# An adaLN block with sliding-window attention and a token MLP: Q's parity copies of two token groups by DMA, K1 and Q2 a group ahead, 20 more token blocks of B1 inside attention

## The chip, the cores and the metric

The kernel runs on one core of one Trainium2 chip. The metric is the device time of one execution in microseconds (us); the median of several executions stands for a kernel. The engines are TensorE (PE; PEld is its weight load), VectorE (DVE), ScalarE (ACT), GpSimd (POOL) and SyncE (SP), which here only issues DMAs.

## The reference

`x` is 2048 tokens by 512 features, bf16. A modulation vector gives six rows of 512.

```
sa, ca, ga, sb, cb, gb = split(silu(c) @ w_mod)
h = layernorm(x) * (1 + ca) + sa
q, k, v = split(h @ wqkv)                 # 32 heads of 16
p = softmax(q k^T * 16**-0.5, only 0 <= query - key < 256)
x = x + ga * ((p v) @ wo)
h = layernorm(x) * (1 + cb) + sb
u = gelu(layernorm(h)^T @ w1 + b1)        # mixes tokens: w1 is 2048 x 1792
x = x + gb * (u @ w2 + b2)^T              # w2 is 1792 x 2048
```

## The kernel before, in words

**Stages.** A prologue makes the modulation and the first projections. Attention follows, then the token MLP: "B1" multiplies the normalized rows `hb` with `w1`, "y" multiplies the result with `w2`.

**Attention** is cut into four token groups `tg` of 512 tokens, each into four head blocks `g8` of 8 heads, each into five units: 80 units in all, 20 per token group (`ul` = 0 to 19). Four units of a head block (k = 0, 1, 3, 4; kind A) hold one parity of the heads and half of the keys' pieces; unit k = 2 (kind C) holds the pieces that fill the rest of the window. In each unit TensorE makes scores into PSUM (`emit_scores`, L548, L555, L575, L585), ScalarE turns them into exponentials in two instructions (`emit_exp`, L598), and TensorE multiplies these with V (`av_a`, L609, from `VaugT`; `av_c`, L623, from `Vc`, after units k = 2 and 4). VectorE transposes the products (L655), GpSimd and VectorE normalize them into `OTd` (`norm_rest`).

**Q in two copies.** A 32-row piece of Q holds two heads of 16 rows. `QT[tg][g8]` has two copies of Q, one with only the even heads' rows, one with only the odd heads', zeros elsewhere. `qk_group` (L292 to L317) evacuates Q from PSUM into `qs` (VectorE, L309), then two masked copies are made from it (L313, GpSimd but for one). `qpool` has two buffers for each `g8`.

**Dense groups.** Beside its own products TensorE gets at most one dense group per unit, of 16 matmuls (`dense`, L267), through one PSUM buffer `dn`: projections of V, Q and K, transposes of the normalized x, the output projection of a token block (`wo_group`), and parts of B1 (`part_group`). `plan(tg)` (L760) lays each group on a unit: `at[ul]`. Token group tg's own V blocks 2 and 3 come in units 0 and 1, its K and Q of head blocks 1 to 3 in units 2 to 8; the next token group's transposes, first Q and K and V blocks in units 11 to 18; the `wo` groups of the previous token group's four blocks in units 6, 7, 9 and 10. Behind a `wo` group, `ln23` gives three steps for VectorE and GpSimd that end in `hb[tb]`. Steps of this kind wait in `chains`; `fill` puts them between VectorE's fixed work by the planner's costs in `clock`, which also follows GpSimd.

**Parts of B1 in attention.** `part_group(fc, k)` multiplies four token blocks (4k to 4k + 3) of `hb` with the `w1` columns of chunk `fc` (128 of the 1792). `PART = (6, 7, 8, 9)`: these four chunks get their token blocks 0 to 7 in units 12 to 19 of token group 3, and the sum is kept in `part[fc]` in SBUF. After attention they start at token block 8 (L1047), and `emit_gelu` adds the part (L973). The other chunks do all 16 token blocks after attention (`emit_b1_group0_sc`, L961, for chunks 0 to 5; L1050 for the rest).

**Order in one unit** `u` (L881 to L914): first half's exponential; scores of unit u + 1; the products of unit u - 1, if these close a head block's half (k = 2 or 4); the dense group; the second exponential; the group's evacuation (`evac`); the other products; at last `at_unit`, which issues the unit's DMAs. Every engine works through its own list in this order.

**DMAs.** All are issued by SyncE, in program order. `copies_for` (L637) copies V for head block g8 from `VaugT` into the other 64 partitions of `Vc`, three copies each (L633), SBUF to SBUF; `at_unit` issues them for head block 0 in unit 0, and for blocks 1, 2 and 3 in units 3, 4 and 5. From unit 2 of token group 1 on, each unit issues one half row block of `w1` into `w1a` (20 loads for `NA` = 10 token blocks; `paced`, L408). The other token blocks (`w1b`, L946) and `w2` (L948) are loaded when attention's SBUF comes free.

Of the kernel before, what the change touches and what calls it, by code (L numbers as in the profile page):

```python
# [8 lines left out]
DT = mybir.dt  # L9
# [3 lines left out]
P = 128  # L13
# [3 lines left out]
DH = 16  # L17
# [3 lines left out]
ND = D // P  # L21
NF = F // P
EPS = 1e-5
SCORE_SCALE = DH ** -0.5
NA = 10
LIVE = 4
SLACK = 0.3

# [2 lines left out]
def kernel(  # L31
# [25 lines left out]
    dma = nc.sync  # L57
# [33 lines left out]
    hbpool = ctx.enter_context(tc.tile_pool(name="hbpool", bufs=1))  # L91
    hb = [hbpool.tile([P, D], DT.bfloat16, name=f"hb_{t}") for t in range(NT)]
    opool = ctx.enter_context(tc.tile_pool(name="opool", bufs=2))

    PART = (6, 7, 8, 9)
    ppool = ctx.enter_context(tc.tile_pool(name="ppool", bufs=1))
    part = {fc: ppool.tile([P, D], DT.float32, name=f"part{fc}") for fc in PART}
    wqpool = tc.alloc_tile_pool(name="wqpool", bufs=1)
# [66 lines left out]
    build_masks()  # L165


    qpool = tc.alloc_tile_pool(name="qpool", bufs=2)
    kpool = tc.alloc_tile_pool(name="kpool", bufs=1)
    vpool = tc.alloc_tile_pool(name="vpool", bufs=1)  # L170
    qspool = tc.alloc_tile_pool(name="qspool", bufs=2)
# [7 lines left out]
    QT = [[None] * ND for _ in range(NG)]  # L179
    KT = [[None] * ND for _ in range(NG)]  # L180
    VaugT = [None] * NG
    OTd = [[None] * ND for _ in range(NG)]
# [10 lines left out]
    nc.gpsimd.memset(ones[:], 1.0)  # L193


    for tg in range(NG):
        VaugT[tg] = Vring[tg % 2]
        for g8 in range(ND):
            KT[tg][g8] = Kring[tg % 2][:, g8, :]

# [91 lines left out]
    def qk_group(tg, g8, kind, pool):  # L292
        col0 = g8 * P + (D if kind == "k" else 0)

        def mms():
            pq = pool.tile([P, 4 * P], DT.float32, name="dn")
            for dc in range(ND):
                dense(
                    pq, lhsT=wqkv[:, dc, col0 : col0 + P], rhs=h1T[tg][:, dc, :],
                    start=(dc == 0), stop=(dc == ND - 1),  # L300
                )
            return pq

        def evac(pq):
            if kind == "k":
                nc.vector.tensor_copy(out=KT[tg][g8], in_=pq[:])  # L306
                return
            qs = qspool.tile([P, 4 * P], DT.bfloat16, name="qs")
            nc.vector.tensor_copy(out=qs[:], in_=pq[:])  # L309
            QT[tg][g8] = qpool.tile([P, 2, 4 * P], DT.bfloat16, name=f"QT{g8}")  # L310
            for n, m in enumerate((mask_even, mask_odd)):
                eng = nc.vector if (tg, g8, n) == (0, 1, 0) else nc.gpsimd
                eng.tensor_scalar(  # L313
                    out=QT[tg][g8][:, n, :], in0=qs[:], scalar1=m[:], scalar2=0.0, op0=ALU.mult, op1=ALU.add,
                )
            return 0.7 if (tg, g8) == (0, 1) else 1.4
        return mms, evac, (1.05 if (tg, g8, kind) == (0, 1, "q") else 0.7)  # L317
# [70 lines left out]
    with tc.manual_schedule():  # L388
# [6 lines left out]
            out=spread[:].rearrange("p (a b) -> p a b", a=4),  # L395
            in_=identity[0:32, 0:32].unsqueeze(1).to_broadcast([32, 4, 32]),
# [52 lines left out]
        for lo, hi, in_ in (  # L449
# [3 lines left out]
                out=mask_q[:, lo:hi, :], in_=in_.to_broadcast([P, hi - lo, 64]), func=ACT.Copy,  # L453
            )
        for half in range(2):
            part64 = slice(64 - 64 * half, 128 - 64 * half)
            nc.scalar.activation(
                out=Vc[half][part64, :, 0:8, :], func=ACT.Copy,
                in_=zero[part64, 0 : 8 * 2 * DH].rearrange("p (h d) -> p h d", d=2 * DH)
# [32 lines left out]
        for dc in range(ND):  # L492
            if dc < 2:
                nc.vector.tensor_scalar(
                    out=h1T[0][:, dc, :], in0=pts[dc], scalar1=modFM[:, 4 + dc : 5 + dc],
                    scalar2=modFM[:, dc : dc + 1], op0=ALU.mult, op1=ALU.add,
                )
            else:
                nc.scalar.activation(
                    out=h1T[0][:, dc, :], in_=pts[dc], func=ACT.Identity,  # L500
# [4 lines left out]
        for dc in (0, 2, 1, 3):  # L505
            for ps, col0 in ((pq, 0), (pk, D)):
                dense(
                    ps, lhsT=wqkv[:, dc, col0 : col0 + P], rhs=h1T[0][:, dc, :],
                    start=(dc == 0), stop=(dc == ND - 1),
                )  # L510
        QT[0][0] = qpool.tile([P, 2, 4 * P], DT.bfloat16, name="QT0")

        def q_half(n, m, lo, hi):
            nc.vector.tensor_scalar(
# [9 lines left out]
        mms, evac, _ = v_group(0, 0, ps_po, "po")  # L524
# [135 lines left out]
        def norm_rest(tg, g8):  # L660
            t2v = state["t2"][:].rearrange("p a (b c) -> p a b c", c=32)
            m = npool.tile([P, 4 * P], DT.bfloat16, name="merge")

            def quotient():
                zr = npool.tile([P, 2, 16, 1], DT.float32, name="zr")
                nc.vector.reciprocal(out=zr[:], in_=t2v[:, :, :, DH : DH + 1])  # L666
                nc.gpsimd.tensor_tensor(  # L667
                    out=m[:].rearrange("p (b a d) -> p a b d", a=2, d=DH), in0=t2v[:, :, :, 0:DH],
                    in1=zr[:].to_broadcast([P, 2, 16, DH]), op=ALU.mult,
                )  # L670
                return 1.06

            def back():
                OTd[tg][g8] = opool.tile([P, 4 * P], DT.bfloat16, name=f"OTd{g8}")
                nc.vector.transpose(out=OTd[tg][g8][:], in_=m[:])
            return [(quotient, 0.36), (back, 0.72)]

# [60 lines left out]


        def part_group(fc, k):  # L740
            def mms():
                assert done >= set(range(4 * k, 4 * k + 4))
                if k == 0:
                    part[fc, "ps"] = ps_dn.tile([P, D], DT.float32, name="dn")
                for sc in range(4 * k, 4 * k + 4):
                    dense(
                        part[fc, "ps"], lhsT=w1box["a"][:, sc, fc * P : (fc + 1) * P], rhs=hb[sc][:],
                        start=(sc == 0), stop=(sc == 7),
                    )
                return part[fc, "ps"]  # L750

            def evac(ps):
                if k == 1:
                    nc.vector.tensor_copy(out=part[fc][:], in_=ps[:])
            return mms, evac, 0.7 * k


        wo_next = iter(range(12))
# [1 line left out]
        def plan(tg):  # L760
            at, then = {}, {}

            def lay(ul, group):
                assert ul not in at, (tg, ul)
                at[ul] = group

            def qk(ul, g, g8, kind):
                lay(ul, qk_group(g, g8, kind, ps_dn))

            for n in (2, 3):  # L770
                lay(n - 2, v_group(tg, n, ps_dn))
            if tg == 0:
                for ul, g8, kind in ((2, 1, "q"), (3, 1, "k"), (4, 2, "q"), (5, 2, "k"), (6, 3, "q"), (7, 3, "k")):
                    qk(ul, tg, g8, kind)
                lay(8, bias_group(ps_dn))
                lay(13, bc_group(ps_dn))
                then[18] = [(lambda g=g: fold_wod(g), 0.0) for g in range(ND)]
            else:
                for ul, g8, kind in ((2, 1, "k"), (3, 2, "q"), (4, 2, "k"), (5, 3, "q"), (8, 3, "k")):
                    qk(ul, tg, g8, kind)  # L780
                for ul in (6, 7, 9, 10):
                    tb = next(wo_next)
                    lay(ul, wo_group(tb, ps_dn))
                    then[ul] = ln23(tb)
            if tg + 1 < NG:
                t0, t1, q0, v0, k0, q1, v1 = (10, 11, 12, 16, 14, 15, 18) if tg == 0 else (11, 12, 13, 14, 15, 17, 18)
                lay(t0, transpose_group(tg + 1, 0, ps_dn))
                lay(t1, transpose_group(tg + 1, 1, ps_dn))
                lay(v0, v_group(tg + 1, 0, ps_dn))
                lay(v1, v_group(tg + 1, 1, ps_dn))  # L790
                for ul, g8, kind in ((q0, 0, "q"), (k0, 0, "k"), (q1, 1, "q")):
                    qk(ul, tg + 1, g8, kind)
            else:
                for n, fc in enumerate(PART):
                    for k in range(2):
                        lay(12 + 2 * n + k, part_group(fc, k))
            return at, then
# [79 lines left out]
        mms, evac, _ = v_group(0, 1, ps_dn)  # L877
# [3 lines left out]
        for u, (tg, g8, k) in enumerate(units):  # L881
            ul = 5 * g8 + k
# [150 lines left out]
    with tc.tile_pool(name="gtmp", bufs=2) as gtmp:  # L1033
        for i, fc in enumerate(fgroups[1]):
            emit_gelu(pu1, i, fc, gtmp)
        pu1pool.release()
        for i, fc in enumerate(fgroups[0]):
            emit_gelu(pu0, i, fc, gtmp)
        ps_u = [
            tc.alloc_tile_pool(name=f"ps_u{n}", bufs=1, space=bass.MemoryType.PSUM, side="right")  # L1040
            for n in range(2)
        ]
        for n, fg in enumerate(fgroups[2:]):
            pu = ps_u[n % 2].tile([P, 2, D], DT.float32, name=f"pu{n % 2}")
            for sc in range(NT):
                for i, fc in enumerate(fg):
                    s0 = 8 if fc in PART else 0  # L1047
                    if sc < s0:
                        continue
                    nc.tensor.matmul(  # L1050
                        pu[:, i, :], lhsT=w1_of(sc, fc), rhs=hb[sc][:],
                        start=(sc == s0), stop=(sc == NT - 1),
                    )
            for i, fc in enumerate(fg):
                emit_gelu(pu, i, fc, gtmp)
        ps_u[1].release()
        ps_u[0].release()
    pu0pool.release()

    with tc.tile_pool(name="ftmp", bufs=3) as ftmp, tc.tile_pool(  # L1060
        name="ps_y0", bufs=4, space=bass.MemoryType.PSUM
# [61 lines left out]
```

## Time and profile before

| | |
|---|---|
| time, median of 3 runs | 265.92 us (264.77 to 267.12) |
| the profiled execution: its own time | 264.77 us |
| its span, first to last instruction | 263.0 us |
| busy, share of the span: PE / DVE / ACT / POOL | 92% / 64% / 62% / 49% |
| mean granted TensorE clock | 0.993 |
| token group 0 of attention | 13.6 to 50.7 us |
| token group 1 | 50.7 to 88.4 us |
| token group 2 | 88.4 to 127.05 us |
| token group 3 | 127.05 to 165.3 us |
| B1 after attention | 165.3 to 211.2 us |
| y | 211.2 to 263 us |

The token groups are cut where ScalarE begins the first exponential of each (40 exponentials per group). In the profile a line such as L598 is a line of the kernel; "out<-in" names the tiles; "[0.47 <-ACT et L598]" behind an instruction is the idle time of its engine ahead of it and what ended it. A busy TensorE is not one at its peak, since matmuls overlap. DMA-issuing instructions do not count as busy, so SyncE's queue (SPq) has views of its own.

### The profile page before, as it was taken

Reading aid. Unit: us, or ns where it says so; the run is one execution under the profiler, and the core shown is the slowest. Engines: PE = TensorE matmul, PEld = TensorE weight load, DVE = VectorE, ACT = ScalarE, POOL = GpSimd, SP = SyncE. Lnnn points to the kernel's source line nnn. Section 1 sums busy time; section 2 is a strip of 40 time slices with the busy share of each in tenths; the row PEclk is TensorE's granted clock in tenths of the full one; section 3 lists DMA queues with packets and bytes.
Section 4 is the critical chain, followed back from the end, with each engine's and each line's share of the span. In section 5 each row is a group of like instructions: output and inputs, shape, how many; then the busy total and the mean of one; then the engine's idle time right before and its main releaser. Section 6 shows DMA issues by size and latency. Waiting matters only on the chain.

```text
span 263.0 us, 11079 instructions
## 1 busy us (share of the span) xinstructions
PE 240.8 (92%) x4923; PEld 129.6 (49%) x4933; DVE 167.2 (64%) x353; ACT 164.3 (62%) x193; POOL 128.6 (49%) x218
## 2 busy tenths in 40 slices
PE   6988798899998879989899899999999999999994
PEld 2544455455555545555456455444444444444443
DVE  6678868875798697898786877789411001423444
ACT  6688998999999989999999999100082110000000
POOL 6104943699269998898995498954200000000000
PEclk9999979999999999999999999999999999999999
DMA  5949962134744342000122000999800000202021
GB/s 168 340 143 250 245 215 79 47 89 123 224 130 133 110 129 73 6 2 5 32 75 53 5 2 24 333 417 414 356 3 0 2 0 0 80 2 80 20 101 40
DMA packets 26084, 29.95 MB, mean 114 GB/s; under 512 B 3252, under 2 KB 23476, under 8 KB 26036
## 3 DMA queue, kind: packets, MB, share of 16 engines
q1 hardware_dynamic: 26036, 29.25, 35.4%
q8 instruction: 38, 0.62, 1.0%
q14 instruction: 10, 0.08, 0.1%
HBM read 22.55 MB, written 2.23 MB: 94 GB/s over the span
## 4 chain that ended last, share of the span: by engine, by line
PE 70%; DVE 18%; ACT 5%; issue 3%; DMA 2%; SPq 1%; ACTq 0%; DVEq 0%
PE dn L271 19%; PE py L1086 18%; PE pu L1050 8%; PE pu L964 7%; PE pss L548 5%; ACT et L598 5%; PE po L609 4%; PE po L623 3%; DVE t L655 3%; DVE qs L309 3%; DVE VaugT L287 2%; DMA wmod<-in_w_mod_dram 2%; PE pss L555 2%; DVE KT L306 2%; DVE x L370 1%
## 5 line engine op out<-in xcount | busy, mean ns | idle before, releaser
L598 ACT ACTIVATE et<-pss 128x1024 bf16<-128x1024 f32 (+1 forms) x160 | 143.8, 995 | 6.4 <-PE pss L555 5.1
L1086 PE MATMUL py<-guT,w2r 128*128 128x512 bf16 (+1 forms) x234 | 48.3, 366 | 0.2
L1065 DVE SCALAR_TENSOR_TENSOR o<-py,bFM,bc 128x512 bf16<-128x512 f32 (+1 forms) x17 | 11.7, 715 | 44.4 <-PE py L1086 44.4
L271 PE MATMUL dn<-h1T,wqkv 128*32 128x512 bf16 x496 | 33.1, 381 | 3.9 <-DVE VaugT L287 1.3
L1086 PEld LDWEIGHTS <-w2r 128*128 128x128 bf16 x238 | 23.3, 98 | 25.3
L548 PE MATMUL pss<-QT,KT 32*128 32x64 bf16 (+2 forms) x704 | 28.9, 238 | 5.8 <-ACT et L598 4.8
L655 DVE STREAM_TRANSPOSE t<-po 128x512 f32<-128x512 f32 x32 | 22.8, 711 | 11.4 <-PE po L623 11.2
L208 POOL TENSOR_TENSOR ln_rstd<-ln_ve,mhalf 128x1 f32<-128x1 f32 (+1 forms) x40 | 24.1, 602 | 5.7 <-DVE ln_ve L204 2.6
L204 POOL TENSOR_SCALAR ln_ve<-ln_mv 128x1 f32<-128x1 f32 (+1 forms) x38 | 9.1, 240 | 34.7 <-DVE ln_mv L226 17.6
L548 PEld LDWEIGHTS <-KT 32*128 32x128 bf16 x704 | 15.4, 92 | 21.3 <-issue 11.1
L609 PE MATMUL po<-et,VaugT 128*32 128x64 bf16 (+2 forms) x704 | 25.1, 241 | 0.0
L609 PEld LDWEIGHTS <-VaugT 128*32 128x32 bf16 x704 | 17.2, 96 | 11.0 <-issue 2.1
L271 PEld LDWEIGHTS <-wqkv 128*32 128x32 bf16 x512 | 13.1, 95 | 13.5 <-issue 6.0
L555 PE MATMUL pss<-mask_q,mask_k 32*128 32x256 bf16 (+1 forms) x256 | 19.2, 263 | 0.0
L667 POOL TENSOR_TENSOR merge<-t,zr 128x512 bf16<-128x512 f32 x16 | 17.0, 1060 | 3.2 <-DVE zr L666 3.2
L271 PE MATMUL dn<-wqkv,h1T 128*32 128x512 bf16 x240 | 15.7, 380 | 2.2 <-DVE VaugT L287 1.2
L975 ACT ACT_TABLE_LOAD x1 | 1.3, 1283 | 24.9 <-PE pu L964 24.9
L699 POOL TENSOR_TENSOR h<-h,bc 128x512 bf16<-128x512 bf16 x12 | 14.0, 1166 | 3.5 <-DVE h L695 3.5
L271 PE MATMUL dn<-wod,OTd 128*32 128x512 bf16 x192 | 12.6, 381 | 2.0 <-DVE KT L306 1.0
L700 POOL TENSOR_TENSOR h<-h,bc 128x512 bf16<-128x512 bf16 x12 | 13.9, 1155 | 0.9
L964 PE MATMUL pu<-hb,w1a 128*128 128x512 bf16 x58 | 13.2, 379 | 0.2 <-issue 0.2
L623 PE MATMUL po<-et,Vc 128*32 128x64 bf16 x960 | 13.0, 194 | 0.0
(113 smaller groups left out, 363.7 us busy)
## 6 DMA issues: line engine op xcount, KB each, us to landing
w2r<-in_B_w_dram SPq DMA_DIRECT2D x14, 512.0 KB, 10.1
w1a<-in_B_w_dram SPq DMA_DIRECT2D x20, 224.0 KB, 3.3
w1b<-in_B_w_dram SPq DMA_DIRECT2D x6, 448.0 KB, 7.5
Vc<-VaugT SPq DMA_DIRECT2D x32, 64.0 KB, 2.3
wmod<-in_w_mod_dram SPq DMA_DIRECT2D x8, 256.0 KB, 5.1
out_dram<-otile SPq DMA_DIRECT2D x15, 128.0 KB, 1.7
x<-in_A_x_dram SPq DMA_DIRECT2D x6, 256.0 KB, 4.2
Vc<-VaugT SPq DMA_DIRECT2D x12, 128.0 KB, 3.6
```

The source lines that it names most:

```text
L208: nc.gpsimd.tensor_tensor(out=r[:], in0=ve[:], in1=mhalf[:, 0:n], op=ALU.pow)
L271: nc.tensor.matmul(out[cols, :], lhsT=lhsT[:, cols], rhs=rhs, start=start, stop=stop, tile_position=(0, 32 * j), skip_group_check=True,)
L548: nc.tensor.matmul(pss[j // 2][:, j % 2, c0 : c0 + nq], lhsT=keys(kb, g8)[rows[j], k0 : k0 + P], rhs=QT[tg][g8][rows[j], par, q0 : q0 + nq ...
L555: nc.tensor.matmul(pss[j // 2][:, j % 2, :].rearrange("p (a r) -> p a r", a=2)[:, 0:n, :] .rearrange("p a (b q) -> p a b q", q=64)[:, :, 0 ...
L598: act = nc.scalar.activation(out=et[:, :, 0:n], in_=state.pop((u, a))[:, :, 0:n], func=ACT.Exp, scale=SCORE_SCALE,)
L609: nc.tensor.matmul(state["po"][32 * j : 32 * j + 32, q0 : q0 + nq], lhsT=VaugT[kb // 4][:, kb % 4, 8 * g8 + 2 * j + par, :], rhs=state["e" ...
L623: nc.tensor.matmul(state["po"][32 * j : 32 * j + 32, q0 : q0 + 64], lhsT=Vc[half][:, b, 8 * g8 + 2 * j + par, :], rhs=state["e", tg, g8, 2 ...
L655: nc.vector.transpose(out=state["t2"][:, par, :], in_=state["po"][:])
L667: nc.gpsimd.tensor_tensor(out=m[:].rearrange("p (b a d) -> p a b d", a=2, d=DH), in0=t2v[:, :, :, 0:DH], in1=zr[:].to_broadcast([P, 2, 16, ...
L964: nc.tensor.matmul(pu[:, i, :], lhsT=w1_of(sc, fc), rhs=hb[sc][:], start=(sc == 0), stop=(sc == NT - 1),)
L1050: nc.tensor.matmul(pu[:, i, :], lhsT=w1_of(sc, fc), rhs=hb[sc][:], start=(sc == s0), stop=(sc == NT - 1),)
L1086: nc.tensor.matmul(pys[n][:, 0 : hi - lo], lhsT=w2r[:, fc, tb * P : (tb + 1) * P], rhs=guT[fc][:, lo:hi], start=(fc == 0), stop=(fc == NF ...
```

## The change

`QT` becomes a ring of two fixed sets of tiles (token groups 0 and 2 share one, 1 and 3 the other), and for token groups 2 and 3 each Q group fills its two copies by eight DMAs from `qs`, 16 rows of 1 KB each, into the rows where the zeros of the earlier group do not lie; GpSimd's two masked copies go. For token groups 2 and 3, K of head block 1 and Q of head block 2 are made a token group earlier, in units 16 and 19. The `wo` groups of token groups 2 and 3 move to units 5, 6, 7 and 9. Four more chunks get parts: 10, 11 and 13 of four token blocks, 12 of eight, in units 8 and 10 of token group 2 and 8, 10 and 11 of token group 3. `NA` becomes 8, so 16 instead of 20 loads of `w1a` and 8 instead of 6 of `w1b`. `OTd` has one buffer instead of two for head blocks 2 and 3.

```diff
-NA = 10
+NA = 8
...
-    PART = (6, 7, 8, 9)
+    PART = {6: 8, 7: 8, 8: 8, 9: 8, 10: 4, 11: 4, 12: 8, 13: 4}
...
-    qpool = tc.alloc_tile_pool(name="qpool", bufs=2)
+    qpool = tc.alloc_tile_pool(name="qpool", bufs=1)
...
+    Qring = [[qpool.tile([P, 2, 4 * P], DT.bfloat16, name=f"QT{r}{g8}") for g8 in range(ND)] for r in range(2)]
+
     for tg in range(NG):
         VaugT[tg] = Vring[tg % 2]
+        for g8 in range(ND):
+            QT[tg][g8] = Qring[tg % 2][g8]
...
             nc.vector.tensor_copy(out=qs[:], in_=pq[:])
-            QT[tg][g8] = qpool.tile([P, 2, 4 * P], DT.bfloat16, name=f"QT{g8}")
+            if tg >= 2:
+
+                for row in range(0, P, DH):
+                    head = slice(row, row + DH)
+                    dma.dma_start(out=QT[tg][g8][head, row // DH % 2, :], in_=qs[head, :])
+                return
             for n, m in enumerate((mask_even, mask_odd)):
...
-                OTd[tg][g8] = opool.tile([P, 4 * P], DT.bfloat16, name=f"OTd{g8}")
+                OTd[tg][g8] = (opool if g8 < 2 else opool1).tile([P, 4 * P], DT.bfloat16, name=f"OTd{g8}")
...
+            last = k == PART[fc] // 4 - 1
+
...
-                        start=(sc == 0), stop=(sc == 7),
+                        start=(sc == 0), stop=(sc == PART[fc] - 1),
...
-                if k == 1:
+                if last:
                     nc.vector.tensor_copy(out=part[fc][:], in_=ps[:])
-            return mms, evac, 0.7 * k
+            return mms, evac, 0.7 * last
...
-                for ul, g8, kind in ((2, 1, "k"), (3, 2, "q"), (4, 2, "k"), (5, 3, "q"), (8, 3, "k")):
+                if tg == 1:
+                    order = ((2, 1, "k"), (3, 2, "q"), (4, 2, "k"), (5, 3, "q"), (8, 3, "k"))
+                else:
+                    order = ((2, 2, "k"), (3, 3, "q"), (4, 3, "k"))
+                for ul, g8, kind in order:
                     qk(ul, tg, g8, kind)
-                for ul in (6, 7, 9, 10):
+                for ul, fc, k in {2: ((8, 10, 0), (10, 11, 0)), 3: ((8, 13, 0), (10, 12, 0), (11, 12, 1))}.get(tg, ()):
+                    lay(ul, part_group(fc, k))
+                for ul in (6, 7, 9, 10) if tg == 1 else (5, 6, 7, 9):
                     tb = next(wo_next)
...
                 for ul, g8, kind in ((q0, 0, "q"), (k0, 0, "k"), (q1, 1, "q")):
                     qk(ul, tg + 1, g8, kind)
+                if tg:
+                    qk(16, tg + 1, 1, "k")
+                    qk(19, tg + 1, 2, "q")
             else:
-                for n, fc in enumerate(PART):
+                for n, fc in enumerate((6, 7, 8, 9)):
...
-                    s0 = 8 if fc in PART else 0
+                    s0 = PART.get(fc, 0)
```

More of the change, by code (lines that the diff above doesn't have):

```diff
@@ L93 @@
     opool = ctx.enter_context(tc.tile_pool(name="opool", bufs=2))
-    PART = (6, 7, 8, 9)
+    opool1 = ctx.enter_context(tc.tile_pool(name="opool1", bufs=1))
+    PART = {6: 8, 7: 8, 8: 8, 9: 8, 10: 4, 11: 4, 12: 8, 13: 4}
     ppool = ctx.enter_context(tc.tile_pool(name="ppool", bufs=1))
@@ L510 @@
                 )
-        QT[0][0] = qpool.tile([P, 2, 4 * P], DT.bfloat16, name="QT0")
         def q_half(n, m, lo, hi):
```

## The prediction

> **What bounds the kernel now.** I read the page first (busy shares, groups, issues), then the table of stretches, with attention cut at its four token groups (13.6, 50.7, 88.4, 127.05 and 165.3 us), then the order of time on TensorE and on the DMA queue at a group boundary.
>
> The stretches, with a row each for token groups 1, 2 and 3:
>
> ```profile
> core 0: us, PE busy (x) PEld busy (x) DVE busy (x) ACT busy (x) POOL busy (x), PEclk, DMA share, GB/s
> 50.70:88.40 37.70, 34.20 (x1128) 20.51 (x1127) 29.72 (x58) 37.29 (x42) 26.97 (x41) 1.00 0.47 133
> 88.40:127.05 38.65, 34.18 (x1144) 20.69 (x1136) 31.66 (x59) 37.56 (x42) 34.73 (x57) 1.00 0.18 48
> 127.05:165.30 38.25, 35.14 (x1166) 21.13 (x1155) 28.59 (x56) 37.55 (x41) 29.48 (x44) 1.00 0.15 41
> ```
>
> In attention ScalarE works 112.4 of 114.6 us: the exponentials bound it, one per 0.933 us where nothing disturbs them (20 in 18.66 us), 9.33 us per five units. TensorE is close behind. Where it gets a dense group in each unit, five units take it 9.62 us (group starts 151.73 to 161.35), more than ScalarE; units without a group (16 and 19 in groups 1 and 2, 11 in group 3) let it catch up. Its order of time there:
>
> ```profile
> 121.93 0.28 PE L548 MATMUL pss<-QT,KT 32*128 32x256 bf16 x2
> 122.68 0.31 PE L548 MATMUL pss<-QT,KT 32*128 32x256 bf16 x8 [0.47 <-ACT et L598]
> 127.26 0.28 PE L548 MATMUL pss<-QT,KT 32*128 32x256 bf16 x2
> 128.18 0.37 PE L548 MATMUL pss<-QT,KT 32*128 32x256 bf16 x8 [0.63 <-ACT et L598]
> 129.08 1.06 PE L271 MATMUL dn<-wqkv,h1T 128*32 128x512 bf16 x16
> 134.62 0.42 PE L623 MATMUL po<-et,Vc 128*32 128x64 bf16 x32
> ```
>
> The scores after an empty unit wait for ScalarE. The last line is the first product that reads Vc in group 3, 7.6 us into the group. From 165.5 us on TensorE alone bounds (chain of waits: 49 matmuls of L1050 in 10.74 us, 0.2192 us each).
>
> The queue that the change loads is SyncE's. First its issues at that boundary in order of time, then issues by line, with minimum, median and maximum in ns:
>
> ```profile
> 127.10 12.64 SPq L633 DMA_DIRECT2D Vc<-VaugT  x12
> 163.05 3.52 SPq L946 DMA_DIRECT2D w1b<-in_B_w_dram  x6
> ```
>
> ```profile
> L633 SPq DMA_DIRECT2D Vc<-VaugT x44: 590/597/1761, 15.4 to 139.1; - x44
> L948 SPq DMA_DIRECT2D w2r<-in_B_w_dram x14: 327/328/836, 166.8 to 181.4; - x14
> L437 SPq DMA_DIRECT2D b<-in_B_b_dram x1: 436/436/436, 10.8 to 10.8; - x1
> L1073 SPq DMA_DIRECT2D out_dram<-otile x17: 332/333/385, 224.6 to 260.4; - x17
> ```
>
> An issue costs the queue 0.33 us or more however little it moves (L437: 4 KB), and 0.59 us from SBUF to SBUF, the same for 64 and 128 KB. Three Vc copies stand 0.647 us apart (1.94 us at 50.38).
>
> **The change part by part.**
>
> *Tail.* Twenty matmuls leave L1050: 20 x 0.2192 = 4.38 us, all on the path, since TensorE has no gap there: -4.38. The four extra additions of parts (0.685 us each, L973) and their activations lie beside matmuls: the last two feed W2's chunks 12 and 13, read 48 matmuls (10.5 us) into the y stage. With NA 8, w1b has 8 loads. It still starts after the last scores (163.05 us) and moves 8 x 0.459 = 3.67 MB; at the rates of slices 25 to 27 (24, 333, 417 GB/s) it is in by 174, and token block 8 is reached near 180. The W2 load ends 2.2 us later, near 193, and is wanted near 207. Both cost nothing; without that cover of 6 and 14 us, the lateness itself.
>
> *Start of the tail.* The last merge (167.40) waits 0.26 us for GpSimd, the last OTd for two bn_stats on VectorE; wo groups a unit earlier and a lighter GpSimd should give -0.3 (0 to -1.6).
>
> *Filling the empty units.* Five groups more, 0.98 us of TensorE's queue each (153.80 to 154.78): +4.9. Undisturbed scores take 0.44 us of the queue (115.17 to 115.61). In groups 1 and 2 those behind the empty units take 1.19, 0.63, 0.61 and 1.35, 2.02 us too much together; in group 3 0.75 + 0.19 + 0.17 = 1.11. The groups fill 5.15 us of waiting. Against that, with one PSUM buffer, a group in each unit waits for VectorE's evacuation 0.18 + 0.24 us per five units; three refilled stretches add some 1.0. Sum +0.75; bounds 0 (all hidden) and +4.9 (nothing hidden). The three or four new evacuations (0.69) fit in VectorE's 82% (31.66 of 38.65). Units 8 and 10 of group 2 need blocks 0 to 3 of hb: the last is ready at 105.7, the group in unit 8 starts at 106.40, a cover of 0.7 us that the lighter GpSimd widens.
>
> *GpSimd.* Sixteen copies of 0.69 us go, 11.1 us; it was at 34.73 of 38.65 us in group 2. That is off the path, but VectorE is slow beside it: L695 takes 540 ns in attention, the same operation 396 (L1000) in the tail, and L289 451 with a minimum of 219; together (12 x 0.144 + 8 x 0.232) 3.6 us in groups 1 to 3. GpSimd loses 11.1 of its 91.2 us there, 12%: -0.4 (0 to -1.3, where the VaugT waits of 0.27 and 0.94 us at group 2's start go). [...]
>
> *SyncE's queue, the deciding part.* Each Q group of token groups 2 and 3 issues eight copies, SBUF to SBUF, 64 in all. Each queue that is passed: nothing on GpSimd waits; on SyncE the copies stand ahead of Vc's. The Q in unit 17 (Q1) and the Q now in unit 19 (Q2) come right before the three Vc copies of unit 0; the Q in unit 3 (Q3) right before the three of head block 1. TensorE's queue needs the first three at the product of unit 2, the second three at that of unit 7; behind these stand the dense group, the next products and the next scores, so ScalarE runs dry.
>
> Let s be the spacing of Q copies. No row shows 16 partitions from SBUF to SBUF. Below: 0.327 + 0.05 = 0.38. Above: Vc's 0.647. I take 0.60: the nearest rows are the SBUF-to-SBUF ones, at 0.59 whatever their bytes; the simple pattern may save 0.03 to 0.04 (0.367 for two-block loads, 0.33 for plain ones).
>
> - First stall. Q2's group starts at G; its evacuation ends at G + 1.05 + 0.05 + 0.69 = G + 1.8. From G to the first Vc product: 0.87 + 0.33 + 0.44 + 0.46 of queue, then the 5.54 us from 129.08 to 134.62: G + 7.64. Margin 5.85 us. Needed: eight copies 8s = 4.8, two Vc copies 1.29, landing of the third 2.2 (2.0 to 2.3 by the issue rows): 8.29. Q1's eight copies begin two full units earlier (3.91 us, 151.73 to 155.64) and take 4.8: 0.9 of backlog. Stall: 0.9 + 8.29 - 5.85 = 3.3 us.
> - Second stall. From the first Vc product X: qs is ready at X + 2.14 (136.76), the third copy lands at X + 2.14 + 8.29 = X + 10.4, wanted at X + 9.75 (144.37): 0.7 us.
>
> Together 4.0 us per boundary, two boundaries (into groups 2 and 3): 8.0, and 0.4 for the w1a load that group 1 issues between Q1 and Q2: +8.4. TensorE, now full, cannot win it back. With s = 0.65 it is +10.8, with s = 0.38 +1.4. The Q copies themselves are in time: those of unit 13 land near 124.2, wanted at 126.2.
>
> [...]
>
> **Sum:** -4.38 - 0.3 + 0.75 - 0.4 + 8.4 = +4.1 us. The profiled execution took 264.77 us (span 263.0 and 1.77 around it), so 268.9. It is the fastest of the three shown, 1.15 below their median of 265.92; on that scale 270.0. I put 269.4 between.
>
> **Rivals.**
> - *The other side: cheap issues.* If s is at most 0.45, the eight copies take 3.6 us at most, Q1 leaves no backlog, and the stall per boundary is 0.7 to 1.3 us. Sum -2.9 to -1.8: 262 to 264, faster by some 1%. For it: issues of 0.33 to 0.44 for every transfer with DRAM at one end. Against: all 46 SBUF-to-SBUF issues take 0.59 or more. It decides from s = 0.51, where the stalls (4.2 us) equal what the tail and GpSimd give.
> - *In between,* s of 0.46 to 0.53: 264 to 266.
> - *TensorE becomes the bound of attention as well:* the five groups cost their 4.9 in full, 4.15 more than in the sum: 273.5. For it: 9.62 against 9.33 us per five units. Against: the 5.15 us of waits that they fill.
> - *Vc is wanted later than I think,* because TensorE or VectorE is late anyhow (in group 2 that product came at 96.66, 8.3 us in): no stall, everything hidden: 264.77 - 4.3 = 260.4.
>
> **How the numbers follow.** Forecast (s from 0.54 to 0.65, 266.5 to 272.5): 0.52; TensorE bound on top: 0.10; in between 0.15; cheap issues 0.17; no stall 0.06. The range 262.0 to 273.5 leaves out the last case, the lower end of the cheap one and the upper end of the bound one, some 0.17. About 1% (2.7 us) is what a measurement of this kernel can tell from no change. Slower than 268.6: most of the forecast and the bound case, 0.53. Faster than 263.2: 0.21. Within: 0.26.
>
> **What would show it.** In the profile after: Q copies as SBUF-to-SBUF issues of 0.55 to 0.59 us (right) or 0.33 to 0.4 (wrong); TensorE waiting 3 us for a DMA of Vc at the first L623 of groups 2 and 3, with ScalarE idle as long; groups 2 and 3 some 42 us long, group 1 near 38; L1050 down by 20 matmuls; no w1b wait. Groups 2 and 3 within 39 us would prove the queue's part wrong; longer ones without a DMA wait would point to TensorE or VectorE.

## The result and the profile after

The changed kernel takes 283.24 us (median of 4 runs, 282.24 to 283.70) against 265.37 before (4 runs): a ratio of 1.0657, 95% interval 1.0595 to 1.0719. It is slower, as forecast, but by 18 us where some 4 were forecast, and outside the range (262.0 to 273.5). Here and below, medians, ranges and ratios leave out slow runs, more than 1.5% above the fastest of the same kernel (four of ten in the run e2 below, three of ten in e3). Each ratio is to the kernel before as timed beside that run (medians 265.0 to 265.8).

The profiled execution took 283.1 us (span 281.4). By stages, cut where ScalarE begins the first exponential of a token group, and at the first matmul of y:

| stage | before, us | after, us | difference |
|---|---|---|---|
| up to token group 1 | 50.6 | 52.0 | +1.4 |
| token group 1 | 37.8 | 38.25 | +0.45 |
| token group 2 | 38.7 | 49.15 | +10.5 |
| token group 3 | 38.25 | 49.0 | +10.75 |
| B1 after attention | 45.7 | 41.2 | -4.5 |
| y | 52.0 | 51.8 | -0.2 |

The first row need be no effect of the change: in the experiments below, which alter nothing there, it lies between 50.3 and 51.8. So the tail gave what it should, and token groups 2 and 3 took 21 us. Their rows of the stretches, after, with the columns as in the prediction:

```profile
90.25:139.40 49.15, 38.23 (x1168) 22.55 (x1168) 32.19 (x64) 37.99 (x42) 30.39 (x49) 0.90 0.18 47
139.40:188.40 49.00, 38.87 (x1198) 22.59 (x1198) 29.56 (x58) 38.17 (x41) 26.79 (x40) 0.93 0.15 40
```

ScalarE, busy but for 1.1 and 0.7 us of these groups before, now stands idle for 11.2 and 10.8 us. The TensorE clock, 1.00 before, is 0.90 and 0.93 there; TensorE is busy for 4.1 and 3.7 us more than before, of which 1.2 and 1.3 us come with the added groups (run e1 below). TensorE's order of time shows what it waits for: the first two lines of each group are the first product with Vc, the rest the second one.

```profile
103.39 0.24 PE L634 MATMUL po<-et,Vc 128*32 128x64 bf16 x4 [5.56 <-DMA Vc<-VaugT]
104.78 0.56 PE L634 MATMUL po<-et,Vc 128*32 128x64 bf16 x28 [1.15 <-DMA Vc<-VaugT]
118.47 0.39 PE L634 MATMUL po<-et,Vc 128*32 128x64 bf16 x28 [1.91 <-DMA Vc<-VaugT]
152.11 0.25 PE L634 MATMUL po<-et,Vc 128*32 128x64 bf16 x4 [4.98 <-DMA Vc<-VaugT]
153.79 0.57 PE L634 MATMUL po<-et,Vc 128*32 128x64 bf16 x28 [1.43 <-DMA Vc<-VaugT]
166.36 0.21 PE L634 MATMUL po<-et,Vc 128*32 128x64 bf16 x4 [1.27 <-DMA Vc<-VaugT]
```

Before, the line 134.62 had no wait. Now there are 8.6 us of waits in group 2 and 7.9 in group 3 (the last of it, 0.23 us, at 166.80), at exactly the two places of the prediction. The cause stands in SyncE's queue, after, at both boundaries, with the issues of L321 over the run:

```profile
80.82 6.10 SPq L321 DMA_DIRECT2D QT<-qs  x8
87.02 1.95 SPq L420 DMA_DIRECT2D w1a<-in_B_w_dram  x4
89.06 5.25 SPq L321 DMA_DIRECT2D QT<-qs  x8
94.40 1.11 SPq L420 DMA_DIRECT2D w1a<-in_B_w_dram  x1
95.62 5.52 SPq L321 DMA_DIRECT2D QT<-qs  x8
101.24 2.04 SPq L644 DMA_DIRECT2D Vc<-VaugT  x3
130.00 19.87 SPq L321 DMA_DIRECT2D QT<-qs  x24
149.98 2.36 SPq L644 DMA_DIRECT2D Vc<-VaugT  x3
```

```profile
L321 SPq DMA_DIRECT2D QT<-qs x64: 507/587/1521, 80.8 to 162.2; - x64
140.58 0.69 DVE L316 CAST qs<-dn 128x512 bf16<-128x512 f32 x1 [0.33 <-PE dn L278]
```

At the second boundary the 24 copies of three Q groups fill the queue for 20 us with one gap of 1.05 us (136.57 to 137.62, between Q0's copies and Q1's). Q2 is ready at 141.27 (the second line's end); Q1's copies hold the queue for 6.3 us, so Q2's get it at 144.03, and the Vc copies, which before began with the token group, begin at 149.98.

### The profile page after: what moved, and what is told of

It is laid out like the page before. It is cut to its first block, busy times and chain, and to the rows that moved or that the text cites. A ratio compares the mean times of both kernels' runs of the same rounds, so it can differ in the third digit from the quotient of the medians.

```text
span 281.4 us, 11295 instructions
## 1 busy us (share of the span) xinstructions
PE 245.7 (87%) x4993; PEld 131.7 (47%) x4993; DVE 171.0 (61%) x361; ACT 165.5 (59%) x193; POOL 118.0 (42%) x202
## 4 chain that ended last, share of the span: by engine, by line
PE 65%; DVE 15%; DMA 6%; SPq 6%; issue 3%; ACT 2%; POOL 2%; DVEq 0%; ACTq 0%; POOLq 0%
PE dn L278 17%; PE py L1108 17%; PE pu L986 7%; PE pu L1072 6%; PE pss L559 4%; DMA Vc<-VaugT 3%; PE po L620 3%; SPq L321 3%; PE po L634 3%; DVE t L666 3%; ACT et L609 2%; DMA wmod<-in_w_mod_dram 2%; DVE VaugT L294 2%; DVE KT L313 2%; PE dn L260 2%
## 5 line engine op out<-in xcount | busy, mean ns | idle before, releaser
L278 PE MATMUL dn<-h1T,wqkv 128*32 128x512 bf16 x496 | 36.1, 410 | 4.1 <-DVE VaugT L294 1.1
L559 PE MATMUL pss<-QT,KT 32*128 32x64 bf16 (+2 forms) x704 | 27.7, 241 | 3.1 <-ACT et L609 2.1
L634 PE MATMUL po<-et,Vc 128*32 128x64 bf16 x960 | 14.1, 197 | 16.5 <-DMA Vc<-VaugT 16.5
L559 PEld LDWEIGHTS <-KT 32*128 32x128 bf16 x704 | 14.7, 93 | 18.7 <-issue 10.7
L620 PEld LDWEIGHTS <-VaugT 128*32 128x32 bf16 x704 | 18.1, 97 | 11.0 <-issue 1.4
L278 PEld LDWEIGHTS <-wqkv 128*32 128x32 bf16 x512 | 14.1, 100 | 15.6 <-issue 8.4
L634 PEld LDWEIGHTS <-Vc 128*32 128x32 bf16 x960 | 10.2, 98 | 19.3 <-DMA Vc<-VaugT 17.6
L566 PE MATMUL pss<-mask_q,mask_k 32*128 32x256 bf16 (+1 forms) x256 | 18.8, 266 | 0.0
L278 PE MATMUL dn<-wqkv,h1T 128*32 128x512 bf16 x240 | 15.7, 380 | 1.9 <-DVE VaugT L294 0.9
L710 POOL TENSOR_TENSOR h<-h,bc 128x512 bf16<-128x512 bf16 x12 | 13.9, 1157 | 7.3 <-DVE h L706 7.3
L995 DVE TENSOR_TENSOR gelu_a<-pu,part 128x512 f32<-128x512 f32 x8 | 5.2, 686 | 16.4 <-PE pu L1072 16.4
```

The lines of the kernel that those rows point to most:

```text
L278: nc.tensor.matmul(out[cols, :], lhsT=lhsT[:, cols], rhs=rhs, start=start, stop=stop, tile_position=(0, 32 * j), skip_group_check=True,)
L559: nc.tensor.matmul(pss[j // 2][:, j % 2, c0 : c0 + nq], lhsT=keys(kb, g8)[rows[j], k0 : k0 + P], rhs=QT[tg][g8][rows[j], par, q0 : q0 + nq ...
L566: nc.tensor.matmul(pss[j // 2][:, j % 2, :].rearrange("p (a r) -> p a r", a=2)[:, 0:n, :] .rearrange("p a (b q) -> p a b q", q=64)[:, :, 0 ...
L620: nc.tensor.matmul(state["po"][32 * j : 32 * j + 32, q0 : q0 + nq], lhsT=VaugT[kb // 4][:, kb % 4, 8 * g8 + 2 * j + par, :], rhs=state["e" ...
L634: nc.tensor.matmul(state["po"][32 * j : 32 * j + 32, q0 : q0 + 64], lhsT=Vc[half][:, b, 8 * g8 + 2 * j + par, :], rhs=state["e", tg, g8, 2 ...
```

## The experiments

Theory Q: the Q copies stand ahead of the Vc copies in SyncE's queue, TensorE waits for Vc, and its clock halves meanwhile (0.50 in the profile). Rivals: TensorE overfull with dense groups (D); the small DMAs harmful in themselves, wherever they stand (L).

### The copies on GpSimd again

```diff
-            if tg >= 2:
-                for row in range(0, P, DH):
-                    ...
-                return
```

> The changed kernel with Q's two copies made by masked copies on GpSimd again in all token groups; K1 and Q2 a group ahead and the 20 token blocks in attention stay. Theory Q (the Q copies stand ahead of the Vc copies on SyncE's queue, TensorE waits for Vc, and its clock halves in the wait): no wait for a DMA of Vc is left, the tail's 4.7 us stay won, filling the empty units costs 0.8: 265.4 - 4.7 + 0.8 = 261.5 us, up to 263.5 if GpSimd, back at 35 of 38.6 us, delays VectorE. Rival D (five more dense groups make TensorE the bound of attention): at least 266 us, token groups 1 to 3 over 39 us each without any wait for a DMA.

Measured 261.26 us (run e1), ratio to before 0.9834 (0.9808 to 0.9860): 1.7% faster than before. Its stretches of token groups 1 to 3:

```profile
50.78:88.97 38.19, 34.78 (x1136) 21.07 (x1133) 30.57 (x58) 37.69 (x41) 27.19 (x42) 1.00 0.44 126
88.97:128.01 39.04, 35.40 (x1168) 21.65 (x1168) 34.09 (x64) 37.78 (x40) 35.76 (x56) 1.00 0.12 29
128.01:166.60 38.59, 36.42 (x1198) 22.11 (x1198) 29.65 (x57) 37.81 (x41) 31.98 (x49) 1.00 0.15 36
```

With all five added dense groups in, attention's groups 1 to 3 take 115.8 us against 114.7 before. Rival D falls: filling the empty units costs 1.1 us, the tail gives 4.5. GpSimd, at 35.8 of 39.0 us, delays nothing that can be told from the time. The whole loss of 22 us belongs to the copies by DMA.

### The same DMAs in another order: Vc ahead

```diff
-                for row in range(0, P, DH):
...
+                def copies():
+                    for row in range(0, P, DH):
...
+                held.append(copies)
...
                 copies_for(tg, max(ul - 2, 0))
+            while held and ul not in (3, 4, 19):
+                held.pop(0)()
```

> The changed kernel with the Q copies held back: those of unit 19 are issued behind the Vc copies of unit 0, those of unit 3 behind the Vc copies of unit 5; same DMAs, other order. Theory Q: the eight copies of unit 17 still take 6 us of the queue and end 4.5 us into the token group, so the third Vc copy lands near 8.0 us where it is wanted at 7.9: a wait under 0.6 us, no half clock: 261.5 to 262.5 us. Rival L (64 small DMAs cost in themselves: late landing, waits on their semaphores by TensorE): 268 us or more, with waits of the scores for QT.

Measured 267.3 us (run e2), with a wide spread (264.16 to 267.88), ratio 1.0051 (1.0014 to 1.0088). Of the 22 us that the copies cost, 16 are gone, but not all. The second version, e2b, swaps Q1 and K1 as well, so that Q1 is made in unit 16:

```diff
-                t0, t1, q0, v0, k0, q1, v1 = (10, 11, 12, 16, 14, 15, 18) if tg == 0 else (11, 12, 13, 14, 15, 17, 18)
+                t0, t1, q0, v0, k0, q1, v1 = (10, 11, 12, 16, 14, 15, 18) if tg == 0 else (11, 12, 13, 14, 15, 16, 18)
...
-                    qk(16, tg + 1, 1, "k")
+                    qk(17, tg + 1, 1, "k")
```

> As the run before (Vc copies ahead of the held Q copies), and Q of head block 1 in unit 16, K of head block 1 in unit 17 (swapped), so the queue is free 1.9 us earlier. Theory Q: no wait for Vc at all: 261 us (260.3 to 262). Rival L: 268 us or more. If theory Q holds but the waits were not at the edge, both runs agree within 0.5 us.

Measured 266.90 us (264.54 to 267.62), ratio 1.0031 (1.0002 to 1.0060). Neither expectation of 261 to 262.5 came true. The waits for Vc in the order of time, first of e2, then of e2b:

```profile
98.94 0.21 PE L637 MATMUL po<-et,Vc 128*32 128x64 bf16 x4 [3.02 <-DMA Vc<-VaugT]
140.85 0.39 PE L637 MATMUL po<-et,Vc 128*32 128x64 bf16 x28 [1.94 <-DMA Vc<-VaugT]
```

```profile
100.19 0.88 PE L637 MATMUL po<-et,Vc 128*32 128x64 bf16 x32 [3.29 <-DMA Vc<-VaugT]
```

In e2b the boundary into group 3 is free, the one into group 2 is not. There the queue still held the copies of Q0 and Q1 and five w1a loads: from 79.89 to 95.91 us it never stood empty. I had counted Q1's copies alone.

### The queue freed altogether

As e2b, and the w1a loads two per unit, so that they end in unit 9 of group 1:

```diff
-            for sc, n in [x for x in [next(w1box.get("sc", iter(())), None)] if x]:
+            for sc, n in [x for x in [next(w1box.get("sc", iter(())), None) for i in range(2)] if x]:
```

> As e2b (held Q copies, Q of head block 1 in unit 16), and the w1a loads two per unit, so that they end in unit 9 of token group 1 and no longer stand between the Q copies. In e2b only group 1's end had a wait (3.4 us for Vc and 0.8 for QT, then 6.8 us of half clock), behind 15.7 us of queue. Theory Q: no wait for Vc at either boundary: 261 to 262 us, the same as the run with the copies on GpSimd, though all 64 copies go by DMA. If the DMAs cost anything in themselves: 264 us or more.

Measured 261.42 us (run e6), ratio 0.9830 (0.9786 to 0.9873): 1.7% faster than before. Its queue at the first boundary, and the first product with Vc behind it:

```profile
80.68 12.27 SPq L322 DMA_DIRECT2D QT<-qs  x16
93.05 2.63 SPq L647 DMA_DIRECT2D Vc<-VaugT  x3
95.78 5.64 SPq L322 DMA_DIRECT2D QT<-qs  x8
```

```profile
97.62 0.42 PE L637 MATMUL po<-et,Vc 128*32 128x64 bf16 x32
```

All 64 copies are there, and TensorE no longer waits for Vc, at this boundary or the next. This settles rival L: the same DMAs cost 22 us or nothing, by their places in the queue. Of L's sign there is a trace: the weight loads of the scores wait for QT twice, 0.4 us each, and the time does not show it. The run also shows that the DMAs gain nothing: 261.42 against 261.26 with the copies on GpSimd.

### Half the copies

Even copy by four DMAs, odd copy on GpSimd:

```diff
-                for row in range(0, P, DH):
+                for row in range(0, P, 2 * DH):
+                ...
+                nc.gpsimd.tensor_scalar(out=QT[tg][g8][:, 1, :], in0=qs[:], scalar1=mask_odd[:], ...)
```

> The changed kernel with the even copy of Q by four DMAs and the odd copy by GpSimd (0.69 us): half the issues in the same places of the queue. Theory Q with issues 0.75 us apart: four take 3.0 us, the copies of unit 17 leave no backlog (3.91 us apart), first wait 3.0 + 1.29 + 2.2 - 5.85 = 0.6 us per boundary, no second wait, no half clock: 261.3 (the run with the copies on GpSimd) + 1.3 = 262.6 us, 261.5 to 264.5. If the cost were in proportion to the number of DMAs (64 cost 22 us), 272 us.

Measured 265.13 us (run e3; 263.03 to 266.74), ratio 0.9972 (0.9924 to 1.0021): no difference from before, and 0.6 us over my range. Its waits:

```profile
99.68 0.39 PE L637 MATMUL po<-et,Vc 128*32 128x64 bf16 x28 [1.10 <-DMA Vc<-VaugT]
139.82 0.39 PE L637 MATMUL po<-et,Vc 128*32 128x64 bf16 x28 [1.78 <-DMA Vc<-VaugT]
150.39 0.39 PE L637 MATMUL po<-et,Vc 128*32 128x64 bf16 x28 [0.76 <-DMA Vc<-VaugT]
```

There are 3.6 us of waits where 1.3 were expected, and the time is 2.5 us above the 262.6 of the sum. Yet half the issues took away 18 of the 22 us, not half (272 us): a queue with a due time, not a price per DMA.

### The copies by DMA alone, on the kernel before

```diff
-            QT[tg][g8] = qpool.tile([P, 2, 4 * P], DT.bfloat16, name=f"QT{g8}")
+            if tg >= 2:
+                for row in range(0, P, DH): ...
+                return
```

with the fixed ring of `QT`; nothing else of the change.

> The kernel before with the Q copies of token groups 2 and 3 by DMA alone; K1 and Q2 stay in units 2 and 3, no added token blocks. Theory Q: the copies of units 13 and 17 and group 1's w1a loads stand ahead of the Vc copies of unit 0 (wait 0 to 1.5 us), those of unit 3 ahead of the Vc copies of head block 1 (third copy at X + 11.6, wanted at X + 9.75: 1.9 us): 2 to 3.5 us per boundary, some half clock: 269 to 273 us. If it takes the copies and K1 and Q2 a group ahead together to do harm: 264.5 to 266 us.

Measured 274.84 us (run e5), ratio 1.0355 (1.0290 to 1.0420): 2 us over my range. The waits lie behind the places of the copies here, those in units 13 and 17 (with group 1's w1a loads between them and Vc), and 3 and 5. Those of group 2, in the profiled execution, which is the slowest of the four (277.36 us):

```profile
101.00 0.88 PE L631 MATMUL po<-et,Vc 128*32 128x64 bf16 x32 [3.07 <-DMA Vc<-VaugT]
113.41 0.21 PE L631 MATMUL po<-et,Vc 128*32 128x64 bf16 x4 [1.02 <-DMA Vc<-VaugT]
115.39 0.57 PE L631 MATMUL po<-et,Vc 128*32 128x64 bf16 x28 [1.77 <-DMA Vc<-VaugT]
```

In group 3 two more follow, of 0.85 and 0.83 us, at the second product. So the copies by DMA cost some 9 us alone, and 22 in the changed kernel. There the first product waits 6.7 and 6.4 us, here 3.1 us and not at all. The order of the queue puts that on Q2's copies, right ahead of Vc's; but the filled units differ as well, and no run takes the two apart.

### TensorE kept busy while it waits

The clock of the changed kernel around the first wait of group 2 (2 us stretches; the clock is the last column but two):

```profile
98.00:100.00 2.00, 0.00 (x0) 0.00 (x0) 0.00 (x0) 1.87 (x3) 1.82 (x4) 0.99 0.12 33
100.00:102.00 2.00, 0.00 (x0) 0.00 (x0) 0.00 (x0) 0.00 (x0) 1.76 (x3) 0.50 0.09 24
108.00:110.00 2.00, 2.00 (x28) 0.92 (x20) 0.62 (x2) 1.85 (x2) 0.00 (x0) 0.50 0.06 16
110.00:112.00 2.00, 2.00 (x83) 1.16 (x76) 1.84 (x4) 1.26 (x2) 0.52 (x2) 0.95 0.12 32
```

It falls to 0.50 some 2 us into the wait, which began at 97.83, and comes back only at 110, 5 us after the wait; a dense group takes 1.90 us instead of 1.05 meanwhile. In all that is 10.2 us at half, and 2.1 us without a matmul went ahead of the fall. That matmuls in the wait would keep the clock at 1 was my estimate. In e4, matmuls whose results nobody reads stand ahead of the first product with Vc in groups 2 and 3:

```diff
+            if closes and tg >= 2 and ul == 3:
+                fill_in = ps_dn.tile([P, D], DT.float32, name="dn")
+                for i in range(24):
+                    nc.tensor.matmul(fill_in[:], lhsT=identity[:], rhs=wod[:, i % ND, :], start=True, stop=True)
```

> The changed kernel with 24 added 128x128x512 matmuls (5.3 us, results unread) ahead of the first product with Vc in token groups 2 and 3, where TensorE waits 6.7 and 6.4 us: extra work, no work left out. If the half clock costs time of its own (in the profile the clock was 0.50 for 10.2 and 6.8 us around these waits, of which some 3 and 2 us were work at half speed): the clock stays at 1 and the time falls by 4 to 5 us to 278 to 279.5. If the half clock only fell into waits: unchanged, 283 to 284.

Measured 281.11 us (280.49 to 283.29), ratio 1.0601 (1.0542 to 1.0660): 2 us less, not 4 to 5. The added matmuls (23 of the 24 have a record) and the waits of group 2:

```profile
96.67 5.34 PE L923 MATMUL dn<-wod,identity 128*128 128x512 bf16 x23
103.31 0.21 PE L634 MATMUL po<-et,Vc 128*32 128x64 bf16 x4 [1.29 <-DMA Vc<-VaugT]
104.71 0.39 PE L634 MATMUL po<-et,Vc 128*32 128x64 bf16 x28 [1.19 <-DMA Vc<-VaugT]
115.78 0.21 PE L634 MATMUL po<-et,Vc 128*32 128x64 bf16 x4 [1.54 <-DMA Vc<-VaugT]
116.83 0.39 PE L634 MATMUL po<-et,Vc 128*32 128x64 bf16 x28 [0.84 <-DMA Vc<-VaugT]
```

Group 2 begins 1.3 us earlier here (88.97 against 90.25), by what went ahead of token group 1, so times are compared from fixed points. The second product comes 12.1 us behind the first, 1.6 us sooner than in the changed kernel (13.7), since Q3 is made at full speed (clock 1.00 from 100 to 116). But it now waits 2.4 us instead of 1.9, and the clock halves there (0.50 from 117.1 to 120.5). The first product itself comes 1.2 us later in the group (15.7 us behind its start against 14.5), as the issues ahead of its Vc copies took longer in this execution. So group 2 takes 49.9 us against 49.15; group 3, with no half clock, 47.7 against 49.0. Of the 1.8 us by which the profiled execution is shorter, 1.5 lie ahead of token group 1, where nothing was changed. The last run fills the second place too, with 10 matmuls:

> As e4 (24 added matmuls ahead of the first product with Vc), and 10 more (2.2 us) ahead of the second one, the place where e4's clock still halved in token group 2 (after 1.5 and 0.8 us of wait). In e4 group 3, without any half clock, took 47.7 us against 49.0, and group 2 49.9 against 49.2. If the half clock's price is work at half speed behind the last wait: no half clock now, group 2 also near 47.5 us, the time 278 to 279.5 us. If SyncE's queue alone sets the pace of the two groups: 281 us as before.

Measured 282.18 us (run e7; 279.45 to 283.33), ratio 1.0611 (1.0533 to 1.0689): no gain. Group 2 took 49.9 us, as in e4. The profile still has a half clock, from 106.1 to 109.5, now behind the first wait: the two dense groups there take 1.54 and 1.76 us instead of 1.05. So these two runs show no price of the half clock of its own: what TensorE gains, it spends in part waiting for the next Vc copies, and the queue scatters by as much. The traces of other runs point to a price where the queue is free again afterwards. Groups 1 to 3 of e2b are 5.8 us longer than those of e6, with 3.3 us of waits for Vc and 6.8 us at half clock; those of e3 are 4.5 us longer, with 3.6 us of waits and none at half clock. That compares traces of kernels that differ in more than the clock, so the price stays open.

## Why the prediction was wrong

- **Tail: right.** -4.38 - 0.3 forecast; B1 is shorter by 4.5 us. w1b and W2 cost nothing.
- **Filling the empty units and the lighter GpSimd: right in size.** +0.75 - 0.4 forecast; with the queue out of the way, groups 1 to 3 are 1.1 us (e1) and 0.6 us (e6, 115.35) longer than before. GpSimd's relief gained nothing that can be told from the time (e6 against e1). That VectorE is slow because GpSimd works beside it was my estimate from two rows, and no run shows it apart from other changes; in groups 1 to 3 VectorE is busy for 92.2 us in e6 and 94.3 in e1, GpSimd for 84.1 and 94.9.
- **SyncE's queue: the mechanism right, the size wrong.** Forecast +8.4; the same DMAs in another order are 21.8 us faster (283.24 against 261.42). The step that failed is "I take 0.60" for s, the spacing of the Q copies. The eights of group 2 take 5.3 to 6.1 us, the 24 of the second boundary 18.8 without their gap: 47.5 us for 64, s = 0.74. The bound from above, 0.65, was exceeded too. A single issue is nearly as priced (median 0.587, and some 0.05 to the next), but 11 of the 64 take 0.88 to 1.52 us. With s = 0.74 the prediction's own formulas give stalls of 5.6 and 1.8 us per boundary, 15.1 us with the w1a load's 0.4; the waits measured are 16.5.
- **The trace of before had the sign of it.** The row of L633 in the prediction has a median of 597 ns and a maximum of 1761. Seven of its 44 issues take 1.0 to 1.8 us, so their mean is 0.73 us, 0.78 with the gap to the next. Nine Vc copies from 95.00 take 7.03 us, 0.78 each. I put that down to waits and priced by the minimum, the median and one undisturbed triple. For the rival of cheap issues I read 0.33 to 0.44 for every transfer with DRAM at one end; that holds for most, but four of `wqkv`'s five took 0.50 us or more, and single ones of `w1a` and `w1b` 1.13 and 1.24.
- **The formula of the first stall, with measured terms,** at the second boundary: backlog 144.03 - 141.27 = 2.8, eight copies 5.8, two Vc copies and a gap 1.9, landing 2.05, margin 141.27 to 147.13 = 5.9. Sum 6.7; measured 4.98 + 1.43 = 6.4. Forecast 3.3. The backlog (0.9 forecast) grew most. Here it is Q1's alone: its copies take 6.3 us, and Q2 is ready 3.7 us behind Q1. At the first boundary it is 3.5 us (92.13 to 95.62): Q0's copies and the four w1a loads behind them make Q1's start 0.6 us late, and the w1a load between Q1 and Q2 takes 1.2 us where I had 0.4. The second stall: 1.9 and 1.5 us against 0.7.
- **What was missing:** of the 21.8 us the waits explain 16.5. With them came the half clock (0.50 for 10.2 and 6.8 us), which the prediction did not have, though I expected TensorE to stand still for 3 us (at the first wait of group 2 the clock fell 2.1 us behind the last matmul). From the dense group behind the first product to the one two units on, TensorE takes 5.9 and 5.35 us (105.15 to 111.03, 154.15 to 159.50) against 3.95 before (134.97 to 138.92), 3.3 us more together. That this is an addition and not waiting moved to another place, e4 and e7 do not confirm. The stretches of groups 2 and 3 bear out the split: against e6, TensorE idles 16.0 us more, and the same matmuls (1168 and 1198 in both) keep it busy 5.6 us more.
- **Rivals.** Cheap issues, and Vc wanted later than I think: refuted (no issue under 0.507, waits of 16.5 us). TensorE as a second bound: refuted by e1.

A version that beats both: the change with the copies on GpSimd (261.26 us), or by DMA with the queue in order (261.42).

## What to carry to other kernels

Here a DMA from SBUF to SBUF cost its queue as much for 16 KB as for 64 and 128 KB (medians of 0.59 us for the Q copies and 0.60 for the Vc copies), so copies that look free beside 2 us of latency (medians of 2.6 and 2.1 us from issue to landing) are priced by their number: multiply by the mean spacing of many issues in the trace, not by an undisturbed one. Then list, in issue order, what stands behind them and when it is due; where the queue never empties over several users, as in e2b, the backlog must be counted from the first. Where a transfer is late, look at the order before taking it away: here the order alone was worth 22 us.

## What the runs showed of the hardware

Of the 64 copies of L321, 11 take 0.88 to 1.52 us to issue instead of 0.59; at the second boundary, where the queue hardly empties, it is every fourth or fifth. In the trace of before it is 7 of the 44 Vc copies. Why, these runs do not tell. Eight copies took the queue 5.3 to 6.6 us in the changed kernel, while each landed 1.7 to 3.5 us after its issue.

In attention the half clock came in stretches of 3.41 us (token group 0, before and after), 10.24 and 6.83 us (groups 2 and 3 of the changed kernel). In e4 one of 3.4 us came behind two waits of 1.54 and 0.84 us with a short product between them; the waits of 1.29 and 1.19 us ahead of it had none behind them.
